# Splitting part of two weight loads into 8-partition transfers, and lengthening runs of filler matmuls, in a fused attention and spectral-mixing kernel

## The chip, the cores and the metric

The kernel runs on one core of a Trainium2 chip. The metric is the device time of one execution in microseconds, as the median of several runs. One profiled execution comes with its trace, whose times count from the start of its span.

## The reference, cut to what matters

There are eight batches, a sequence of 576 rows and 512 channels. A linear attention makes `x`; a real Fourier transform over the sequence follows; each of the first 64 modes is multiplied by its own complex 512x512 matrix (`w_r`, `w_i`, in float32); the inverse transform is added, and a channel product with a rectifier closes.

```
x = phi(q) (phi(k)^T v) / (phi(q) . sum phi(k))         # per head, heads joined to 512 channels
X = rfft(x, axis=1)[:, :64]
Yr = Xr @ w_r - Xi @ w_i ;  Yi = Xr @ w_i + Xi @ w_r    # one matrix pair for each of 64 modes
u = x + irfft(Y)
out = u + max(u @ w_ch, 0)
```

The mode matrices are 64 x 2 x 1 MB = 134 MB in HBM, which is most of what the kernel reads.

## The kernel before, in words

**Weights.** Modes are taken in 32 pairs, `p` = 0 to 31. The tile of a pair, `w{p}`, has 128 partitions of 16 x 512 bf16 (16 KB each). Even partitions hold `w_r`, odd ones `w_i`. `w_load(p, half, ...)` issues one transfer from GpSimd's queue for each half: 64 rows of 32 KB float32 in HBM become 64 partitions of 16 KB bf16, so the transfer casts. All such transfers are pinned in program order. Pairs 0 to 4 have buffers of their own or are loaded ahead (`W_KEEP`, `W_PRE`); from pair 5 on, `w_get(p)` asks for one of two buffers, so the load of pair `p` is issued when the products of pair `p-2` have read their buffer. The last pair (`LAST`, 31) is loaded by `w_load_last` as one half after another of each mode, the final quarter in four pieces.

**Products.** `mode_pair(p)` issues 32 matmuls (line 442, `product`) that read `w{p}`, takes the two results out of PSUM to `ys` (lines 452 and 454), runs the work of the slot `(p, "mid")`, turns the rows with `pick_sb` (line 460, `picks`), runs the work of `(p, "end")` and closes with `keep_warm(FILL.get(p, 0))`. `keep_warm(n)` (line 425) issues n matmuls of 128x128 by 512 columns into a scratch bank `zl`; nothing reads their result. Everything on TensorE is pinned, so its order is the program's.

**Slots.** A list `work` is dealt out over the slots: attention rows from pair 5, folding of the first modes' inverse transform (lines 653 to 684) from the end of pair 15, and from the end of pair 27 the "form" work: `form_z` (line 698), `form_y` (line 711) and `fold_lead` (lines 720 to 727). Pair 30 has the first pieces of the output stage (lines 774 and 874).

**The end.** `last_pair()` has the products of mode 62, four fillers, the picks, a copy, more fillers, and then the 32 matmuls of mode 63 (line 504, `y_last`), which read the last transfers' pieces. All of the output stage comes after `y_last`: transposes and products of the last modes (lines 914 and 920), a small transfer into `YZ_all`, then for each pair of output tiles the sums on TensorE (lines 735 and 774), a rectifier on ScalarE (line 784), an addition on VectorE (lines 811 and 816) and a store.

## Time and profile before

| what | value |
|---|---|
| median of 8 runs | 424.48 us (423.62 to 425.51) |
| the profiled execution's own time | 425.13 us, of which its span is 423.3 us |
| the eight runs | 423.62, 423.64, 423.74, 423.90, 425.07, 425.13, 425.38, 425.51 us |
| TensorE busy | 283.3 us, 67% of the span |
| mean granted TensorE clock | 0.75 of full speed |
| packets of GpSimd's DMA queue | 81.47 MB written, 94.0% of 16 engines' span |
| packets of instruction queue q8 | 26 packets, 0.43 MB |
| read from HBM | 163.93 MB |

The weight transfers are listed with the size that arrives (1024 KB); twice that is read. A transfer is spread over DMA engines, and each of the 16 engines adds one mark to the transfer's semaphore; the trace holds the time of every mark, though not the engine's number. A transfer has landed with its sixteenth mark.

### The profile page before, as it was taken

The numbers are of one execution on the slowest core, as the hardware profiler recorded it, in microseconds if no ns is written. First come the engines' busy times: TensorE is split into PE (matmuls) and PEld (weight loads), VectorE is DVE, ScalarE is ACT, GpSimd is POOL, SyncE is SP. The second block draws the span as 40 slices with busy tenths as digits, with TensorE's granted clock in tenths as the row PEclk, the third lists the DMA queues.
The fourth block names the chain that finished last, engine by engine and source line by source line (L and its number), as shares of the span: only waits on it lengthen the run. The fifth ranks groups of instructions, "written<-read, shape, count | busy, mean of one in ns | idle before, by whom it ended". The sixth has DMA issues, their size and how long they took to land.

```text
span 423.3 us, 7890 instructions
## 1 busy us (share of the span) xinstructions
PE 283.3 (67%) x3378; PEld 152.0 (36%) x3378; DVE 215.6 (51%) x447; ACT 161.8 (38%) x253; POOL 56.3 (13%) x99
## 2 busy tenths in 40 slices
PE   0358587768727644444344778888697885999992
PEld 0247366656512322222122333434243332365420
DVE  4599498886103452454444434544263434322794
ACT  4687588754202102000000244444253441231782
POOL 4222124210000100000001001100000000021000
PEclk9999978898555555555555588889698887579998
DMA  9999999999999999999999999999999999987697
GB/s 214 210 209 216 206 221 201 223 211 221 220 216 221 205 218 221 214 212 218 219 214 215 218 215 215 217 219 214 217 215 217 219 211 220 217 171 154 233 404 306
DMA packets 20802, 93.19 MB, mean 220 GB/s; under 512 B 2080, under 2 KB 11168, under 8 KB 16480
## 3 DMA queue, kind: packets, MB, share of 16 engines
q0 software_dynamic: 16512, 81.47, 94.0%
q1 hardware_dynamic: 4256, 11.22, 7.2%
q8 instruction: 26, 0.43, 0.4%
q14 instruction: 8, 0.07, 0.0%
HBM read 163.93 MB, written 9.44 MB: 410 GB/s over the span
## 4 chain that ended last, share of the span: by engine, by line
DMA 62%; PE 23%; DVE 4%; ACT 3%; issue 3%; POOL 2%; DVEq 0%; POOLq 0%; ACTq 0%
DMA w<-in_moe_w_i_dram 47%; PE P L442 8%; DMA pick_sb<-row_pick 8%; DMA k<-in_k_dram 7%; PE acc L735 3%; PE z L698 2%; PE acc L774 2%; ACT ke L213 2%; POOL w L119 1%; PE zl L425 1%; DVE ys L452 1%; PE yp L711 1%; PE yt L460 1%; DVE x L299 1%; ACT qT L249 1%
## 5 line engine op out<-in xcount | busy, mean ns | idle before, releaser
L442 PE MATMUL P<-w,xt_c 64*32 64x512 bf16 (+2 forms) x1000 | 54.2, 567 | 61.5 <-DMA w<-in_moe_w_i_dram 60.1
L452 DVE CAST ys<-P 128x512 f16<-128x512 f32 x32 | 22.1, 692 | 112.5 <-PE P L442 112.5
L454 ACT CAST ys<-P 128x512 f16<-128x512 f32 x31 | 18.2, 586 | 145.8 <-PE P L442 145.8
L119 POOL DMA_DIRECT2D w<-in_moe_w_r_dram x31 | 16.6, 536 | 245.4 <-PE P L442 130.2
L442 PEld LDWEIGHTS <-xt_c 64*32 64x32 bf16 (+2 forms) x1000 | 17.3, 129 | 80.3 <-DMA w<-in_moe_w_i_dram 45.5
L676 PE MATMUL eps<-wch,xTw 128*128 128x512 f16 x144 | 43.6, 433 | 0.0
L165 PEld LDWEIGHTS <-qT 64*128 64x128 f16 (+1 forms) x640 | 23.3, 124 | 49.3 <-issue 27.9
L165 PE MATMUL num<-kv,qT 64*128 64x65 f16 (+1 forms) x320 | 14.3, 217 | 24.7 <-ACT kv L272 12.9
L657 DVE TENSOR_TENSOR x_main<-ya,x_main 128x512 f32<-128x512 f32 x32 | 22.0, 689 | 15.8 <-PE ya L653 15.6
L659 ACT CAST x16w<-x_main 128x512 f16<-128x512 f32 x32 | 19.8, 618 | 24.2 <-DVE x_main L657 23.3
L684 ACT CAST E<-eps 128x512 f16<-128x512 f32 (+1 forms) x40 | 21.2, 541 | 11.0 <-PE eps L676 10.8
L165 PE MATMUL nw<-kv,qT 64*128 64x65 f16 (+1 forms) x320 | 19.0, 240 | 9.5 <-DVE x_tail L620 4.3
L299 DVE TENSOR_TENSOR x<-num,rd 128x512 f16<-128x512 f32 x32 | 22.1, 692 | 1.1
L242 PE MATMUL qTp<-id,qe 128*128 128x128 f16 x144 | 15.0, 287 | 10.1 <-DVE qe L226 9.6
L213 ACT ACTIVATE qe<-q 128x1152 f16<-128x1152 f16 (+1 forms) x16 | 17.9, 1157 | 10.1 <-DMA q<-in_q_dram 10.0
L460 PE MATMUL yt<-pick_sb,ys 128*128 128x16 f16 x252 | 11.6, 174 | 14.1 <-DMA pick_sb<-row_pick 7.5
L249 ACT COPY qT<-qTp 128x1152 f16<-128x1152 f16 x16 | 19.6, 1289 | 0.5 <-PE qTp L242 0.2
L213 ACT ACTIVATE ke<-k 128x1152 f16<-128x1152 f16 x16 | 17.7, 1152 | 4.8 <-DMA k<-in_k_dram 4.8
L784 ACT ACTIVATE acc<-acc 128x512 f32<-128x512 f32 x34 | 18.1, 582 | 2.4 <-PE acc L735 1.2
L676 PEld LDWEIGHTS <-xTw 128*128 128x128 f16 x144 | 14.2, 111 | 12.3 <-issue 5.9
L460 PEld LDWEIGHTS <-ys 128*128 128x128 f16 x252 | 9.6, 101 | 24.5 <-DVE ys L452 15.3
L119 POOL DMA_DIRECT2D w<-in_moe_w_i_dram x31 | 16.8, 541 | 4.6 <-DMA q<-in_q_dram 2.3
(114 smaller groups left out, 466.1 us busy)
## 6 DMA issues: line engine op xcount, KB each, us to landing
w<-in_moe_w_r_dram POOLq DMA_DIRECT2D x31, 1024.0 KB, 12.2
w<-in_moe_w_i_dram POOLq DMA_DIRECT2D x31, 1024.0 KB, 16.6
out_dram<-x_main SPq DMA_DIRECT2D x11, 512.0 KB, 4.0
k<-in_k_dram POOLq DMA_DIRECT2D x8, 576.0 KB, 12.8
v<-in_v_dram POOLq DMA_DIRECT2D x8, 576.0 KB, 14.8
q<-in_q_dram POOLq DMA_DIRECT2D x7, 576.0 KB, 12.8
out_dram<-x_main SPq DMA_DIRECT2D x6, 256.0 KB, 4.1
q<-in_q_dram SPq DMA_DIRECT2D x2, 576.0 KB, 4.6
```

The source lines that it names most:

```text
L119: nc.gpsimd.dma_start(out=w_in[p][half::2], in_=two.rearrange("g (r dc) e -> (g r) dc e", dc=NDW))
L165: mm = nc.tensor.matmul(num[hpo][orow, c0 : c0 + 65], qT[rows, hpp, h2, cols], kv_sb[rows, hpp, h2, :])
L213: pin(nc.scalar.activation(out=ev[:, c], in_=heads(nm, b, c), func=AF.Exp))
L249: nc.scalar.copy(out=qT[:, :, c * NJ : (c + 1) * NJ], in_=qT_ps.rearrange("p j x -> p x j"))
L299: nc.vector.tensor_tensor(out=dst.rearrange("p (o c d) -> p o c d", o=2, c=4), in0=nv[:, :, :, 0:64], in1=rden.unsqueeze(3).broadcast_to([ ...
L442: nc.tensor.matmul(P[c : c + n, :], xt_cols(dc, kk, n), w[rows, dc, :], start=(dc < NDC), stop=(dc >= n_dc - NDC), tile_position=(rows.sta ...
L452: pin(nc.vector.tensor_copy(out=st, in_=P))
L460: nc.tensor.matmul(yt_ps[:, ec, kk % 8, :], st[:, ec * 128 : ec * 128 + 128], pick_sb)
L657: pin(nc.vector.tensor_tensor(out=x, in0=acc, in1=x, op=ALU.add))
L659: pin(nc.scalar.copy(out=x16w[t], in_=x))
L676: nc.tensor.matmul(e_ps, xT[:, c, :], wch16[:, c, :], start=(c == 0), stop=(c == NDC - 1))
L684: pin(nc.scalar.copy(out=dst, in_=e_ps[:, cols]))
```

## The change

In pairs 12 and 22 (`LEVEL`) the `w_r` half is no longer one transfer of 64 rows. It becomes six: rows 1, 3, 5, ... (32 rows of 32 KB); rows 2, 6, 10, ... (16 rows of 32 KB); then twice 8 rows, every eighth from row 0 and then from row 4, each time first the 2 KB at the head of the 8 rows and then the other 30 KB of them. The `w_i` half of those pairs and all other pairs stay. The number of fillers goes up after pairs 20 to 26 (1 to 4), 27 (1 to 7), 29 (2 to 8), 30 (3 to 5), and before `y_last` (6 to 8).

```diff
+    LEVEL = (12, 22)
...
         two = (moe_w_r, moe_w_i)[half][2 * p : 2 * p + 2]
-        pin(
-            nc.gpsimd.dma_start(
-                out=w_in[p][half::2], in_=two.rearrange("g (r dc) e -> (g r) dc e", dc=NDW)
-            )
-        )
+        rows_in = two.rearrange("g (r dc) e -> (g r) dc e", dc=NDW)
+        if half or p not in LEVEL:
+            pin(nc.gpsimd.dma_start(out=w_in[p][half::2], in_=rows_in))
+            return
+        for r0, step in ((1, 2), (2, 4)):
+            pin(nc.gpsimd.dma_start(out=w_in[p][2 * r0 :: 2 * step], in_=rows_in[r0::step]))
+        for j in range(2):
+            for dcs in (slice(0, 1), slice(1, NDW)):
+                dst = w_in[p][8 * j :: 16, dcs]
+                pin(nc.gpsimd.dma_start(out=dst, in_=rows_in[4 * j :: 8, dcs]))
...
-        keep_warm(6)
+        keep_warm(8)
...
-    FILL = {**{p: 1 for p in range(20, 27)}, 27: 1, 28: 1, 29: 2, 30: 3}
+    FILL = {**{p: 4 for p in range(20, 27)}, 27: 7, 28: 1, 29: 8, 30: 5}
```

## The prediction

> **What bounds the kernel now.** I read the page first. The software queue's packets fill 94% of 16 engines' span, and the DMA row stands at 9 until slice 35, where GB/s drops. So up to about 375 us the weight stream is the bound, and the two slices after it are something else. One more row matters: 26 instruction packets on q8, 0.43 MB.

> ```profile
> PEclk9999978898555555555555588889698887579998
> DMA  9999999999999999999999999999999999987697
> GB/s 214 210 209 216 206 221 201 223 211 221 220 216 221 205 218 221 214 212 218 219 214 215 218 215 215 217 219 214 217 215 217 219 211 220 217 171 154 233 404 306
> ...
> q0 software_dynamic: 16512, 81.47, 94.0%
> ...
> q8 instruction: 26, 0.43, 0.4%
> ```

> Then the chain of waits, for who ends last there. Columns: start, length, what.

> ```profile
> 342.47 17.29 DMA w<-in_moe_w_i_dram
> 359.80 1.95 PE P L442 x20
> 361.75 1.92 PE z L698 x8
> ...
> 375.67 1.03 PE P L442 x27
> 376.71 0.62 PE yp L711 x8
> 377.33 0.93 PE z L698 x8
> ...
> 389.54 1.31 PE zl L425 x6
> 390.85 0.92 PE y_last L504 x32
> ```

> w28 lands at 359.76, and from there to 391.77 (end of `y_last`) the chain never leaves TensorE. The windows and POOL's timeline say why that matters:

> ```profile
> 365.00:370.00 5.00, 5.00 (x18) 1.11 (x17) 2.08 (x3) 1.38 (x3) 0.00 (x0) 0.50 1.03 220
> 370.00:375.00 5.00, 5.00 (x27) 2.33 (x26) 1.12 (x2) 1.55 (x3) 0.00 (x0) 0.50 1.03 220
> 375.00:380.00 5.00, 5.00 (x79) 3.46 (x77) 1.45 (x3) 2.12 (x4) 2.12 (x4) 0.97 0.64 120
> ```

> ```profile
> 377.07 0.53 POOL L131 DMA_DIRECT2D w<-in_moe_w_r_dram  x1 [13.91 <-PE P L442]
> ```

> TensorE is full but at half clock until 375.31 (the same 8 matmuls of L698 take 1.92 us before and 0.93 after). w29 lands at 369.41, yet its products run at 375.67, because the form work of pair 28 stands ahead of them. They free the buffer of the last load, so that load is issued only at 377.07, when the stream has run dry: 0.64 DMA share, 120 GB/s.

> **The other half: the 16 engines are not level.** The trace's 16 marks of w30's `w_i` are 375.70, .73, .79, .83, 376.17, .18, .27, then 377.75, then eight from 378.73 to 379.16. At 12 us the same spread was 0.5. The q8 row explains eight of them: 0.4% of 16 x 423.3 us over 26 packets is about 1 us per packet, 24 of these packets lie before 376 us, and eight engines with three each are 3 us late. The engine at 377.75 jumped by about 0.35 four times, each at an 8 KB packet of the other instruction queue. Today the dry spell hides this: everybody restarts at about 379.2, as the early engines wait 3.5 us.

> [...] The trace of before has 16 marks per transfer; it has no transfer of 8 partitions[...]. [...] its clock stretches are multiples of 3.41 us, up after a window of dense matmuls, down after one with about half idle.

> **Part 1, the split.** Rate: w26 and w28 land at 340.31 and 359.76, so four 1024 KB transfers take 19.45 us, 4.86 each; an engine has four 32 KB rows of each, 1.21 us a row. In a split half every engine keeps 2 + 1 rows; of the fourth, eight engines get 2 x 2 KB and the other eight 2 x 30 KB. That is -28 KB or +28 KB, 28/32 x 1.21 = **1.06 us per pair, 2.12 us for two**, opposite in sign. The number of bytes is the same. Ten further transfers bring ten further marks per engine, a 4-byte packet each (22 ns in the trace): 0 to 0.2 us, and I take 0, since the 4.86 us already holds such marks.
> Issue: one issue of 0.53 us becomes six, so GpSimd gives out the `w_i` half 2.65 us later, twice. The cover is the queue itself: pair 12's `w_i`, issued at 186.73, landed at 203.27, and its first bytes were due only after `w_r` at about 198. GpSimd idles 8 us ahead of each pair, and nothing but later loads stands behind it. Its issues reuse eight semaphores: seven issues in a row could wait for the landing eight back (188.76 for pair 12), about when the seventh would go out anyway. Bounds 0 to 2 us, hidden by 9 us; I take 0.
> If the relieved eight are those with q8's packets, w30's marks become: eight at 376.6 to 377.0, seven at 377.8 to 378.4, and the one with the 8 KB packets at 377.75 + 2.12 = **379.87**. That last engine is a price the change doesn't avoid; it is 0.7 us later than the slowest is now.

> **Part 2, the fillers.** A filler takes 0.43 us at half clock, 0.22 at full (L425, six in 1.31). After pairs 20 to 26: 3 more each, 0.65 to 1.3 us, beside waits for weights of 1.4 to 1.6 us; only ahead of pair 27 is the wait as short as 0.36, and there the landing moves up to 0.7 us later as well. Nothing.
> After pair 27: 7 at half clock are 3.0 us from 356.94, so the 2.26 us of idle ahead of w28's products is filled up to about 360. With products (1.95) and `form_z` (1.92) behind it, TensorE is dense for some 7 us where it had 3.9. A whole window fits, so I expect full clock from about 361 (358.5 to 364) and not from 375.31.
> Then the work from 359.80 to 375.67 (15.9 us) shrinks at a ratio of about 0.55 (1.03/1.95, 0.93/1.92) but for the first us, to about 9.5: w29's products at about 370.2, when their last weights land as well. The last load goes out at about 371.5, well ahead of the engines' running dry.
> After pair 29: 6 more at 0.22, 1.3 us; pair 30 and the end: 2 and 2, 0.9 us. Cover: TensorE, 5 us ahead by then, waits for w30 (379.87) and for the last pieces. If the clock stays low this cover is gone, and they are 2.2 us on the path.

> **The sum.** Without a dry spell each engine goes on from its w30 mark. First to last mark of the final load took 9.95 us for an undelayed engine (379.28 by its first row, to 389.23). Slowest: 379.87 + 9.95 = 389.8. A q8 engine with the 25th packet: 378.73 - 2.12 + 0.97 + 9.95 = 387.5. TensorE: w30's products to 381.0, 2.4 us of output work, 5 fillers, mode 62 at about 384.8, its fillers and picks, 8 fillers to 388.3: it waits. `y_last` waits by pieces, so only four of 32 matmuls follow the landing: 390.1, against 391.77 now. The path behind `y_last` is TensorE's and moves along. 425.13 - 1.7 = **423.4 us**. The profiled run is one of the upper four (425.07 to 425.51); the median is 424.48, so against it this is -0.25%. The lower four, 1.5 us below, fit runs in which the clock rose a window or two earlier by luck: I expect such times in all runs, and little more.

> **Rivals.**
> A. *Same direction, more.* If the engine at 377.75 is among the relieved ones, the slowest is at about 378.4, the last landing at 388.4, and TensorE's own path sets `y_last` to 389.0: 425.13 - 2.8 = 422.3. For: engines can't be told apart. Against: it isn't one of q8's eight by the size of its jumps.
> B. *Slower: the tilt goes the wrong way.* If the 30 KB pieces fall on an engine with q8's packets, those go from 379.16 to 381.28. It decides as soon as one engine is later than about 381.2 at w30, for the dry spell that hid it is gone: 381.28 + 9.95 = 391.2, or 391.8 for the one with the 25th packet; `y_last` ends at 392.05: 425.4 us, +0.2% on the median. [...] Against: only the start is against it, as short and long take turns.
> C. *Fillers without the clock.* If no window is dense enough, the form work stays cold: +0.7 for the later w28 and +2.2 for fillers, 428.0. Against: 7 us of dense work is two windows.
> D. *No tilt at all*, if 8 partitions spread over 16 engines. Then the fillers act alone: 378.73 + 0.97 + 9.95 = 389.65, `y_last` to 389.9, 423.3, the same as the main case.

> **How the numbers follow.** Main case and D: 0.50, at 423.4, own range 422.8 to 424.1. A: 0.17. B: 0.25, at 424.9 to 425.8. C: 0.08. Faster means below 423.63, since 0.2% (0.85 us) is about what a measurement of this kernel can tell from no change. Main gives 0.38 faster and 0.12 same, A 0.17 faster, B 0.08 same and 0.17 slower, C 0.08 slower: 0.55, 0.20, 0.25. The range runs from A to the upper end of B, 422.0 to 425.8, and leaves C out.

> **What would show it.** Right: full clock from about 361; the L131 issues at about 371; no DMA share below 0.9 between 375 and 385; L698's eights at 0.93 from pair 28; w30's marks with eight at about 376.8 and one alone near 379.9; TensorE idle ahead of `y_last` on a weight transfer. Wrong: w30's last mark beyond 381 with eight or more there (B); 0.50 clock through 370 (C); 16 marks with the old gap of 3 us (D). Beyond these, a chain that leaves TensorE and the weights after 360 us would break the argument.

## The result and the profile after

The median after is 426.38 us (425.26 to 427.29, 12 runs) against 424.62 (423.30 to 426.03, 33 runs of the kernel before on the same chip): a ratio of 1.0045, interval 1.0031 to 1.0058. The change makes the kernel slower by 0.45%. The profiled execution took 426.24 us with a span of 424.4, against 425.13 and 423.3. The profile of the kernel before is one of its longer executions, so the two spans differ by 1.1 us where the medians differ by 1.76. About 0.3 us of the 1.76 lies behind the span: time less span is 1.74 to 1.87 us in the 176 runs of the kernel before for which both are on record, and 2.16 on average, 2.99 at most, in those of the change. What stands there is in the last section.

Three rows of the page, in 40 slices of the span: the granted TensorE clock, the DMA engines' busy share, and the rate.

```profile
PEclk9999686889955555555555598989798988899997
DMA  9999999999999999999999999999999999996697
GB/s 214 210 208 215 207 220 202 227 208 216 223 211 222 212 212 219 216 218 215 214 215 221 215 212 215 218 217 207 210 218 210 212 221 213 216 205 131 234 402 305
```

The dry spell of slice 35 in the kernel before (171 GB/s) is gone, 205 now, so the fillers' part looks done. The end of the stream is what moved: slice 36 is at 131 where it had 154. The chain of waits from 359.80 us (start, length, what) says why:

```profile
359.80 3.10 PE zl L431 x7
362.90 1.49 PE P L448 x21
...
364.69 0.51 POOL w L121
365.20 18.09 DMA w<-in_moe_w_i_dram
...
383.33 1.10 PE P L448 x27
...
388.59 0.97 PE zl L431 x4
...
389.65 1.74 PE zl L431 x8
...
391.42 1.12 PE y_last L510 x28
...
392.58 0.30 PE y_last L510 x4
```

Before, this chain stayed on TensorE from 359.80 to the end of `y_last` at 391.77, but for 0.43 us of VectorE at 364.15 (`YZ_all`). Now it leaves TensorE for pair 30's `w_i` half, which lands at 383.28 instead of 379.16. The products of pair 30 follow 0.05 us later, the output work and the fillers behind them, and the last fillers end at 391.40. The final piece of weights lands at 392.54 (before 390.33), and `y_last` is over at 392.88. That is 1.1 us later than before, all of the difference of the spans. In the change the 28 products of `y_last` that don't read the final piece end at 392.54 too, so TensorE had no time left over either.

The windows from 365 us (busy time of PE, PEld, DVE, ACT and POOL, then clock, DMA share and GB/s), and POOL's timeline for the issue of the last load:

```profile
365.00:370.00 5.00, 4.48 (x32) 1.93 (x28) 2.76 (x6) 2.28 (x5) 0.73 (x2) 1.00 1.01 213
370.00:375.00 5.00, 5.00 (x71) 3.53 (x72) 1.74 (x4) 2.47 (x5) 0.50 (x1) 1.00 1.03 220
375.00:380.00 5.00, 5.00 (x64) 4.47 (x62) 1.51 (x4) 1.76 (x3) 2.87 (x7) 1.00 0.99 208
```

```profile
374.50 0.52 POOL L137 DMA_DIRECT2D w<-in_moe_w_r_dram  x1 [8.77 <-PE P L448]
```

The clock is full where it was 0.50, and the DMA share of 0.64 between 375 and 380 has become 0.99. The last load goes out at 374.50, not at 377.07. So the stream is fed, and still ends later: some engines have more of it left. The marks of pair 30's `w_i` half show that directly. These are times of the trace's semaphore marks in us, one for each of the 16 engines, in order of time:

```
before  375.70 .73 .79 .83  376.17 .18 .27  377.75  378.73 .82 .85 .86 .92 .99  379.09 .16
after   377.36 .38 .43 .48 .53 .71 .76 .79  378.55  379.29  381.33 .38 .47 .50 .57  383.28
```

The gap between the first mark and the last has grown from 3.46 to 5.93 us, and six engines are beyond 381.3 where none was beyond 379.2. The early engines have gained nothing: they too are 1.7 us later than before.

### The profile page after: what moved, and what is told of

It reads as the page before. It is cut to its first block, busy times and chain, and to the rows that moved or that the text cites. A ratio compares the mean times of both kernels' runs of the same rounds, so it can differ in the third digit from the quotient of the medians.

```text
span 424.4 us, 7982 instructions
## 1 busy us (share of the span) xinstructions
PE 277.4 (65%) x3415; PEld 152.3 (36%) x3415; DVE 215.5 (51%) x447; ACT 161.6 (38%) x253; POOL 61.8 (15%) x109
## 3 DMA queue, kind: packets, MB, share of 16 engines
q0 software_dynamic: 16768, 81.47, 93.9%
## 4 chain that ended last, share of the span: by engine, by line
DMA 66%; PE 19%; DVE 4%; ACT 4%; issue 3%; POOL 2%; DVEq 0%; POOLq 0%; ACTq 0%
DMA w<-in_moe_w_i_dram 48%; DMA pick_sb<-row_pick 8%; PE P L448 8%; DMA k<-in_k_dram 7%; DMA w<-in_moe_w_r_dram 3%; PE acc L741 3%; PE acc L780 2%; PE zl L431 2%; ACT ke L219 2%; POOL w L121 1%; ACT qT L255 1%; PE eps L682 1%; DVE ys L458 1%; DVE x L305 1%; PE yt L466 1%
## 5 line engine op out<-in xcount | busy, mean ns | idle before, releaser
L448 PE MATMUL P<-w,xt_c 64*32 64x512 bf16 (+2 forms) x1000 | 50.6, 534 | 63.7 <-DMA w<-in_moe_w_i_dram 62.3
L121 POOL DMA_DIRECT2D w<-in_moe_w_r_dram x29 | 15.5, 534 | 224.3 <-PE P L448 107.2
L448 PEld LDWEIGHTS <-xt_c 64*32 64x32 bf16 (+2 forms) x1000 | 16.9, 127 | 82.7 <-DMA w<-in_moe_w_i_dram 43.5
L682 PE MATMUL eps<-wch,xTw 128*128 128x512 f16 x144 | 41.4, 416 | 0.0
L248 PEld LDWEIGHTS <-qe 128*128 128x128 f16 x144 | 13.6, 139 | 11.2 <-DVE qe L232 10.0
```

Of the source, the lines that this page charges most:

```text
L248: nc.tensor.transpose(qT_ps[:, j], phi["q", b][:, c, j].rearrange("p o d -> p (o d)"), id16,)
L448: nc.tensor.matmul(P[c : c + n, :], xt_cols(dc, kk, n), w[rows, dc, :], start=(dc < NDC), stop=(dc >= n_dc - NDC), tile_position=(rows.sta ...
L682: nc.tensor.matmul(e_ps, xT[:, c, :], wch16[:, c, :], start=(c == 0), stop=(c == NDC - 1))
```

## The experiments

From the loading of the last pair on, the line numbers of a kernel with the split are six higher than before (L442 becomes L448), those of the turned kernels some more. Comments in the excerpts of code are added here.

**First: the two parts apart, and the order of the short and long pieces.** Four kernels, beside 60 runs of the kernel before (424.98).

The fillers of the change without the split:

```diff
-        keep_warm(6)
+        keep_warm(8)
...
-    FILL = {**{p: 1 for p in range(20, 27)}, 27: 1, 28: 1, 29: 2, 30: 3}
+    FILL = {**{p: 4 for p in range(20, 27)}, 27: 7, 28: 1, 29: 8, 30: 5}
```

> The fillers of the change without the split. Theory T (the split tilts the load the wrong way: its 30 KB pieces fall mostly on engines that also fetch TensorE's instructions; the fillers themselves are good): full clock by about 364 us, w29's products by about 371, no dry spell, w30's last mark at about 379.2 as before, y_last over by about 390, 423.3 us, 1.3 below the kernel before. Rival F (the longer filler runs cost the time, the split does nothing): 426 us or more.

Measured: 423.69 us (423.40 to 425.07, 22 runs, of which 21 are at or below 424.46), ratio 0.9977, interval 0.9968 to 0.9986. This half alone makes the kernel faster, and it is the best version of the study. The profiled execution is the longest of the 22, 425.07 us, but its span, 422.0, is like that of the others (421.6 to 422.4): what is longer lies behind the span. Three views of it: the chain, one window, POOL's timeline.

```profile
357.25 3.10 PE zl L425 x7
360.35 1.85 PE P L442 x23
...
362.49 0.52 POOL w L119
363.01 27.06 DMA w<-in_moe_w_i_dram x2
...
390.11 0.30 PE y_last L504 x4
```

```profile
365.00:370.00 5.00, 5.00 (x40) 2.82 (x40) 2.66 (x5) 2.93 (x5) 0.00 (x0) 1.00 1.03 220
```

```profile
372.30 0.52 POOL L131 DMA_DIRECT2D w<-in_moe_w_r_dram  x1 [8.76 <-PE P L442]
```

From 363.01 us on only weights are on the chain, and TensorE waits for the final piece (390.06). `y_last` is over at 390.41, 1.36 us before the kernel before. The clock is full from 361.9 us.

The split without the fillers, which is the change with the two filler lines put back:

> The split without the additional fillers. Theory T: w30's marks spread over some 6 us as in the changed kernel, the clock rises as late as before, so both prices are paid: w28 about 2.4 us later than before and the form work cold behind it, 426.5 to 427.5 us. Rival F: 424.6, like the kernel before. Rival I (ten more issues and their marks cost the time, whatever engine they use): 426 as well, so this one tells F from the others only.

Measured: 426.30 us (426.18 to 428.03, 7 runs), ratio 1.0045, interval 1.0027 to 1.0063. So the split alone makes the kernel as slow as the change does, and the loss is the split's. The gain of the fillers doesn't show beside it: 1.0045 with them and without, where they give 0.9977 alone. The expectation, 426.5 us or more with both prices paid, was missed a little: in the profiled execution the clock was full from 365.3 us without the added fillers. It shows a second thing: the final piece landed at 391.17 and `y_last` was over at 391.52, before the 391.77 of the kernel before, and yet the span is 424.6. The clock had fallen behind it:

```profile
385.00:390.00 5.00, 3.67 (x25) 1.23 (x23) 1.32 (x2) 0.00 (x0) 0.00 (x0) 1.00 0.76 146
390.00:395.00 5.00, 4.54 (x48) 2.85 (x49) 1.52 (x4) 1.14 (x4) 0.56 (x1) 0.76 0.06 10
```

TensorE was busy for only 3.67 of 5 us while it waited for late weights, and the output stage behind began at half clock (392.6 to 396.0).

The same split with the long pieces ahead of the short ones:

```diff
-            for dcs in (slice(0, 1), slice(1, NDW)):
+            for dcs in (slice(1, NDW), slice(0, 1)):
```

> The change with the 30 KB piece ahead of the 2 KB piece, so that the halves trade places. Theory T with two halves that match the instruction engines exactly: the reverse tilt relieves all eight, 423.4 us. Theory T with a 6 to 2 overlap, as the marks of the changed kernel suggest (six marks about 4 us behind at w30): six relieved, two go to about 381.2 at w30, the last landing 391.2 to 391.8, 425.3 us. Rival I: 426.4, the same as the change.

Measured: 425.34 us (424.58 to 428.10, 22 runs), ratio 1.0021, interval 1.0009 to 1.0033. Only two marks of pair 30's `w_i` are late now (381.22 and 381.55; the others up to 380.29), and the last landing of its profiled execution is at 392.49. The order decides who is loaded, but this order isn't harmless either.

The order short, long, long, short, meant to give every engine one short and one long piece:

```diff
-            for dcs in (slice(0, 1), slice(1, NDW)):
+            for dcs in (slice(0, 1), slice(1, NDW))[:: 1 - 2 * j]:
```

> The change with the order turned round in the second of each two: short, long, long, short. Same transfers, sizes and number of issues, but each half of the engines gets 32 KB, so no tilt. Theory T: marks of w30 as before (last at about 379.2), 423.3 us, like the fillers alone. Rival I: 426.4, like the change. If both halves of every transfer go to the same engines [...], then order doesn't matter: 426.4 here and with the long piece first.

Measured: 424.11 us (423.77 to 425.07, 22 runs), ratio 0.9989, interval 0.9980 to 0.9999. All ten further transfers are there, and the kernel is within 0.42 us of the fillers alone. In the profiled executions `y_last` is over at 390.53 (390.41 in the fillers alone):

```profile
390.23 0.30 PE y_last L510 x4
```

On average the span is 0.28 us longer (422.14 and 421.86), and 0.09 us lies behind it; where in the span the 0.28 go, I haven't located. So the transfers themselves cost little, and the tilt is the loss. The tilt can be read off the next transfer, pair 12's `w_i`, first and last mark in us:

```
fillers alone           201.13   203.24
short long long short   201.11   203.44
short first (change)    200.19   204.34
long first              200.24   204.16
```

Against the even order the change moves the first mark by -0.92 and the last by +0.90.

So the four pieces didn't all go to the same engines, nor each to all of them, or their order could not matter as it does. The marks of the change also fit the eight and eight that part 1 assumed, when no trace had shown it. In its trace a 32 KB row is a packet of 1,227 ns, a 30 KB piece of 1,151 and a 2 KB piece of 96: two short pieces in place of a row are 1.03 us less, two long ones 1.08 us more. From the marks of pair 11's `w_i` (191.49 to 193.54), with 9.75 us for the two transfers up to pair 12's (fitted), eight engines 1.03 us earlier, eight 1.08 us later and one of them another 0.94 us for q8's packet at 197.89, all 16 marks of pair 12's `w_i` (200.19 to 204.34) come out within 0.08 us. On which eight the first piece falls, no run shows.

**Second: turn the halves, and ask what the fillers' parts do.** Four kernels, beside 51 runs of before (424.33). If two rows of the second transfer go out ahead of the 8-row pieces and the other 14 after them, the pieces might begin two engines further on; I assumed so, and no run shows it. Long first:

```diff
-        for r0, step in ((1, 2), (2, 4)):
-            pin(nc.gpsimd.dma_start(out=w_in[p][2 * r0 :: 2 * step], in_=rows_in[r0::step]))
+        part(1, 2, slice(0, NDW))
+        part(2, 4, slice(0, NDW), 10)          # 2 rows
...
+            for dcs in (slice(1, NDW), slice(0, 1)):
+                part(4 * j, 8, dcs)
+        part(10, 4, slice(0, NDW))             # 14 rows
```

> [...] the first two of the 16 rows go out ahead as a transfer of 2 partitions, the other 14 after the short and long ones [...], and the long piece of each two goes first. Theory T2 (the eight instruction engines are neighbours, and the halves of the change miss them by two places, 6 to 2): now all eight are relieved by 2.12 and the other eight loaded. w30's marks: instruction engines about 2.1 earlier against the fillers alone, the engine with the 8 KB packets last but one or last at about 379.7, last landing about 389.6 against 390.06, 423.3 us. Rival (misses by two in the other direction): 4 to 4, spread of marks up to 7 us, last landing 392, 426 us.

Measured: 425.87 us (22 runs), ratio 1.0032, interval 1.0019 to 1.0044. The profile shows a wait that I had not reckoned with here:

```profile
186.18 3.71 POOL L126 DMA_DIRECT2D w<-in_moe_w_r_dram  x7 [8.62 <-PE nw L176]
193.84 0.59 POOL L121 DMA_DIRECT2D w<-in_moe_w_i_dram  x1 [3.95 <-DMA w<-in_moe_w_i_dram]
```

The issue of pair 12's `w_i` is the eighth in a row, and it waits 3.95 us for an earlier transfer's landing. Its first mark comes at 201.65; the engine that was first with the piece before it had been done at 195.37. A transfer of this size takes 4.85 us, so early engines stood still for about 1.4 us at pair 12 (an expectation further down says 1.7). The same edit in pair 12 alone (`LEVEL = (12,)`):

> The same for pair 12 alone, half the tilt. T2: the instruction engine with four packets goes from 4.4 to 3.3 behind the fillers-alone baseline, the engine with the 8 KB packets to 2.8, the last landing to about 389.0, y_last over at about 389.3, 422.6 us: faster than the fillers alone (423.7) by about 1 us. Rival 4 to 4: last landing 391.1, 424.7 us.

Measured: 424.21 us (14 runs), ratio 0.9998, interval 0.9983 to 1.0012: no difference that can be told. The last landing of its profile is 389.87, near neither T2's 389.0 nor the rival's 391.1. And short first in both pairs:

> [...] so under T2 all eight instruction engines get the 30 KB pieces and nobody of them is relieved: eight marks of w30 at 381.3 or later, the one with four packets beyond 382, last landing 391.2 to 392.5, 426 us, like the change (which loads six of them; the slowest one sets the end). Rival 4 to 4: the same time, but four late marks of w30 and not eight. The count of late marks tells the two apart.

Measured: 426.54 us (14 runs), ratio 1.0047, interval 1.0032 to 1.0061, as slow as the change. Pair 30's `w_i` has five late marks (381.18 to 381.38; the next is 378.83), neither the eight of T2 nor the four of the rival. So either the two rows ahead don't move the pieces on by two engines, or the engines with the instruction packets aren't neighbours; the marks, which bear no engine's number, can't tell the two apart.

Fourth, of the fillers only those after pair 27:

```diff
-    FILL = {**{p: 1 for p in range(20, 27)}, 27: 1, 28: 1, 29: 2, 30: 3}
+    FILL = {**{p: 1 for p in range(20, 27)}, 27: 7, 28: 1, 29: 2, 30: 3}
```

> The kernel before with seven fillers after pair 27 instead of one, no other change. If it is these that lift the clock ahead of the form work: full clock by about 364, last load issued by about 373, no dry spell, 423.7 us like all fillers of the change together. If the clock needs the fillers of pairs 20 to 26 or those behind 29 as well: half clock to 375 as before, 425 us or more.

Measured: 424.06 us (423.34 to 425.33, 14 runs), ratio 1.0001, interval 0.9988 to 1.0014. The times fall in two groups, eight at 423.34 to 424.11 and six at 424.57 to 425.33. The profiled execution is of the upper group, and its clock was up early all the same (L131 issued at 371.70, `y_last` over at 390.31). What it lost lies behind; its chain and two windows:

```profile
391.07 0.85 PE zl L920 x4
391.92 0.85 PE z1l L920 x4
...
393.23 1.50 PE acc L735 x4
```

```profile
380.00:385.00 5.00, 3.32 (x27) 0.93 (x19) 0.69 (x1) 0.58 (x1) 0.00 (x0) 1.00 0.99 203
385.00:390.00 5.00, 4.18 (x50) 2.08 (x50) 1.32 (x2) 0.00 (x0) 0.00 (x0) 1.00 0.45 83
```

The same two windows of the fillers alone:

```profile
380.00:385.00 5.00, 4.39 (x54) 1.55 (x53) 0.69 (x1) 0.59 (x1) 0.00 (x0) 1.00 0.99 203
385.00:390.00 5.00, 4.97 (x55) 2.29 (x53) 1.32 (x2) 0.00 (x0) 0.00 (x0) 1.00 0.47 85
```

TensorE was idle a third of the time between 380 and 385 and a sixth between 385 and 390; in the 3.41 us just ahead of the fall (387.41 to 390.82) it was busy 2.44 us. The clock was at half from 390.8 to 394.2. The `zl` group of line 920 took 0.85 us where the fillers alone have 0.44, and the first sums of line 735 took 1.50 where they have 1.02. That fits a use of the fillers after pairs 29 and 30 and before `y_last`: they hold the clock while TensorE waits for weights. It rests on this one profile; no kernel with them and without those of pairs 20 to 26 was run.

**Third: turn the halves without the long queue.** Here 14 rows go ahead of the pieces, and the last two follow pair 12's `w_i`, so only six transfers stand ahead of it. Three kernels, beside 52 runs of before (424.86). Long first, pair 12 alone:

```diff
+        part(0, 1, 2)
+        part(0, 2, 4, stop=58)                 # 14 rows
...
+            for dcs in (slice(1, NDW), slice(0, 1)):
+                part(0, 4 * j, 8, dcs)
...
             part(half, 0, 1)
+            if half and p in LEVEL:
+                part(0, 58, 4)                 # 2 rows, after w_i
```

> Turned the other way: ahead of the long and short pieces 14 of the 16 rows go out, the other 2 after the pair's w_i half[...], and no pair has seven transfers ahead of its w_i (in the turn by +2 the eighth had to wait for a semaphore, w_i was issued at 193.8 and the early engines ran dry for 1.7 us). Long piece first, pair 12 alone. Theory T3 (the turn by +2 gave a 4 to 4 overlap, so the instruction engines are the eight that a turn by -2 meets): all eight relieved by 1.06, the engine with four packets from 4.4 to 3.3 behind the first, last landing at about 389.0 against 390.06 with the fillers alone, 422.7 us, 1 us below them. Rival (the overlap isn't a matter of a turn, the instruction engines aren't neighbours): 4 to 4 or 6 to 2 again, last landing 391.1, 424.7 us.

Measured: 424.51 us (22 runs), ratio 0.9994, interval 0.9984 to 1.0003. Two engines are still 4.7 us behind the first at pair 30, and the last landing is 389.83, again between the two forecasts. In both pairs:

> The same in pairs 12 and 22, the change's full tilt in the right direction. T3: the instruction engines end first, at w30 2.1 earlier than with the fillers alone; the eight others 2.1 later, that with the 8 KB packets last by 1.5 us, at about 379.7; last landing about 389.6, 423.2 us. Rival: spread over 6 us and last landing 392 as in the change, 426 us.

Measured: 425.37 us (22 runs), ratio 1.0028, interval 1.0017 to 1.0039, with a last landing of 391.34. Short first in both pairs:

> The same two pairs with the short piece first, the tilt the wrong way for all eight: T3 expects eight late marks at w30 (the change had six), the early eight within 1 us or, for the one with 8 KB packets, a little behind, last landing 391.5 to 392.5, 426.2 us. Rival: fewer than seven late marks.

Measured: 426.48 us (15 runs), ratio 1.0036, interval 1.0024 to 1.0049. Five marks of pair 30's `w_i` are late (381.38 to 381.55), the other eleven at or before 378.91. Neither way of turning put all eight on one side, so the attempt to aim the tilt failed. Short first costs about the same in all three forms (1.0036 to 1.0047), long first less in each (in the turned forms by 0.67 and 1.11 us, beside the same runs of before); which engines a 2-row or a 14-row transfer takes stays open.

**Fourth: all the added fillers but those after pair 27.** The fillers of the change, no split, `27: 1`; beside 13 runs of before (423.60):

> All additional fillers of the change but those after pair 27, no split: the other half of the run with pair 27's alone. If pair 27's seven lift the clock: half clock to about 375 as before, the form work cold, and the 10 fillers behind it (2.2 us at full clock) on TensorE's path, y_last over at about 394, 426.5 us. If the fillers of pairs 20 to 26 lift it: full clock ahead of 370 and 423.7 us, like all of them.

Measured: 425.72 us (8 runs), ratio 1.0042, interval 1.0018 to 1.0066. Two runs are at 423.40 and 423.84, six at 425.57 to 427.29. The profiled execution is one of the two, with its clock up at 363.1. With pair 27's six added fillers 21 of 22 runs were at or below 424.46; without them six of eight are beyond 425.5. So they matter for the time of most runs. That the six are runs in which the early clock didn't come fits what is on record: their mean granted clock is 0.764 to 0.780, that of the two fast ones 0.790 and 0.793. It is not shown, for no profile of one of the six was taken, and the profile there is has the early clock without pair 27's added fillers. The other fillers then cost less than the 2.2 us reckoned: the median of the six is 425.9, that of the five later runs of the kernel before beside them 425.2.

## Why the prediction was wrong

I forecast 423.4 us as the likeliest, and the median is 426.38, beyond the upper end of 425.8. Rival B, held at 0.25, named the mechanism and the side.

**The step that failed** is the condition in part 1, "If the relieved eight are those with q8's packets". The sum was worked out on that side, though no view of before shows which eight are relieved. What remained as an argument against B was that short and long take turns, which says nothing of that. The runs show the other case. Six of 16 engines were beyond 381.3 at pair 30, and only engines that had been in the late group (about 379.05 with the fillers alone) get there by adding 2.12 us; one of the others would have come to 378 to 380. With the split alone the kernel is at 1.0045, and with the pieces balanced the loss is gone. It is not the clean opposite either, for which rival B's sign asked eight marks beyond 381. Six late marks with short first and two with long first mean that the eight engines of the pieces and the eight of the instruction packets overlap only in part.

**Sized right:** the tilt where it is made. I had 1.06 us per pair and sign; pair 12 shows -0.92 and +0.90 against the even order. B's late marks were to be at 381.28, and five of the six came at 381.33 to 381.57. The issue of six transfers for one was put at nothing, and no gap shows there: the first mark of pair 12's `w_i` is at 201.11 with the even order and at 201.13 with one transfer; after the second split, at pair 22, it is at 298.26 and 298.18.

**Sized wrong:** B's end, `y_last` over at 392.05. B put the engine with the 25th packet of q8 at a last landing of 391.8, which is 378.73 + 2.12 + 0.97 + 9.95, the earliest of the eight. In the profiled execution the late group stood 0.5 to 0.7 us beyond B's 380.85 (378.73 + 2.12) at pair 30, at 381.33 to 381.57, and its engine with that packet (962 ns, at 381.26; I take it to be the one at 383.28) landed last by 1.14 us, at 392.54 against 391.40. That gives 392.88. In the profile of the split alone the 25th packet came later (893 ns, at 385.09), no single engine stands out at the end, and the last landing is 391.17. Which engine the packet meets changes between executions, so in part the size is luck.

**Not foreseen:** the relieved engines lose their relief. I had eight engines gain what eight lose. But a load lands with its last engine, its products wait for that, and the next load waits for the buffer: in the change the last mark of pair 22's `w_i` comes at 304.17, its products start at 304.21, and the load of pair 24 goes out at 306.52. After the second split the marks of pair 23's `w_i` lie 6.66 us apart (306.71 to 313.37); the load of pair 24 (issued at 304.27 with the fillers alone) has its first mark 6.50 us after the one before it, where 4.85 is the pace. The windows of the change and then of the fillers alone, in the same stretches:

```profile
305.00:308.00 3.00, 3.00 (x32) 1.15 (x17) 1.62 (x3) 0.99 (x2) 1.04 (x2) 0.50 0.94 186
...
328.00:333.00 5.00, 4.07 (x36) 2.01 (x41) 2.28 (x5) 2.81 (x5) 0.00 (x0) 1.00 0.94 195
```

```profile
305.00:308.00 3.00, 3.00 (x20) 1.07 (x19) 1.28 (x4) 1.21 (x2) 0.33 (x1) 0.62 0.97 208
...
328.00:333.00 5.00, 4.37 (x52) 2.03 (x51) 2.05 (x4) 2.05 (x5) 0.93 (x2) 1.00 0.99 211
```

The early engines ran dry in small pieces, so at pair 30 all of the stream is late, in the profiles: the first mark by 1.53 us against the fillers alone (377.36 and 375.83), the late group by about 2.4 (381.45 and 379.0).

**Part 2 held for the fillers alone.** Full clock was expected from about 361 us; it came at 361.9 with the fillers alone and at 363.7 with the change. The last load was to go out at about 371.5 (372.30 with the fillers alone, 374.50 in the change, where the stream was late), and rival D, fillers without a tilt, was to give 423.3 us (measured 423.69). That the earlier clock came by luck in the lower group of the kernel before has support, though no profile of that group: of the 60 runs beside the first experiments the 21 below 424.3 us have a mean granted clock of 0.778, the 39 above it 0.762. Rival C, 2.2 us for fillers at a low clock, did not happen in the change.

**One reading of the trace in the prediction was too wide.** It has the clock go up after a window of dense matmuls. In the trace of before TensorE was busy for 92 to 100% of the 3.41 us ahead of each of the 13 rises, and for 0 to 59% of those ahead of each of the 14 falls. But the prediction's own lines show TensorE busy for all of 365 to 375 us and the clock at 0.50 throughout: two whole windows of the clock (3.41 us each), 365.06 to 371.89, were 100% busy and the clock stayed low after each. It rose at 375.31. With the fillers alone the window from 358.46 to 361.88 was 100% busy too, and there it rose. So a window without a gap was not enough; what the kernel before lacked from 365 us on, the runs don't show.

The change is thus two changes of opposite sign that do not add up: the fillers alone are worth -0.23%, close to the forecast -0.25%; the split costs 0.45% without them, and with them it costs their gain besides.

## What to carry to other kernels

A correction that moves load from one group of engines to another needs to know which group it hits; if no view says so, both signs are cases of equal standing, and the order that cancels (short, long, long, short) is the control to run first. With two buffers in rotation the stream here was as late as its latest engine, and what the others gained was given back as soon as they waited for the next issue: pair 24's first mark came 6.50 us after the one before it, at a pace of 4.85. Fillers have to be judged by what the clock does behind them: in the profiles it was full from 361.9 us with all of the added ones and from 375.31 in the kernel before, and its mean from 390 to 395 us was 1.00 with all of them and 0.66 with only those after pair 27. A gain measured alone need not survive beside another change: here 0.9977 alone became 1.0045 beside the split, where the late weights set the end.
